# A gated mix of an S4 convolution and linear attention: key sums through DMA transposes and narrow matmuls, values copied once to bf16, the query normaliser read back repeated from DRAM, the cosine table from ScalarE, and a new order

## The chip, the cores and the metric

One core of a Trainium2 chip. A core has engines with in-order queues of their own: TensorE (PE in the profile; PEld is its weight loads), VectorE (DVE), ScalarE (ACT), GpSimd (POOL) and SyncE (SP, which here issues nearly all DMAs). The metric is device time in microseconds (us) of one execution; the numbers shown are medians over runs. A time in the profile comes from one profiled execution.

## The reference

Two branches read the same `x = A_u` (2,048 positions, 512 channels, bf16) and are mixed by a gate per position:

```python
g = _sigmoid((x * gate_w).sum(-1, keepdims=True))
a = _A_ref(x, A_A_re, A_A_im, A_B_re, A_B_im, A_C_re, A_C_im, A_log_dt, A_Dskip)
b = _B_ref(x, B_wqkv, B_w_phi, B_wo)
return g * a + (1 - g) * b
```

Branch A (`_A_ref`) is an S4 layer: for each channel `d` a kernel `K[d, l] = Re sum_n C[d,n] exp(dt[d] A[d,n] l) dt[d] B[d,n]` over 128 states, a causal convolution of `x` with `K` by FFT of length 4,096, and `+ u * Dskip`. Branch B is linear attention with 32 heads of 16:

```python
phi_q = jnp.concatenate([_softmax(pq, axis=-1), _softmax(-pq, axis=-1)], axis=-1)
phi_k = jnp.concatenate([_softmax(pk, axis=-1), _softmax(-pk, axis=-1)], axis=-1)
kv = jnp.einsum("bhsf,bhsd->bhfd", phi_k, v)
z  = jnp.einsum("bhsf->bhf", phi_k)
num = jnp.einsum("bhqf,bhfd->bhqd", phi_q, kv)
den = jnp.einsum("bhqf,bhf->bhq", phi_q, z)[..., None] + 1e-6
o = num / den
```

and `o @ wo`, where `pq` and `pk` are the queries and keys times a 16 x 16 matrix of each head.

## The kernel before

**The order.** Nothing is scheduled by hand in the text. One `Plan` object (L92) collects the work as nodes: `P.add(engine, cost, function, deps, take, drop)` for a few instructions of one engine, `P.dma(...)` for DMAs that SP issues. The numbers (cost, `move`) served a planner outside the program; in the program the sequence of all nodes is the string `ORDER` (two digits of base 64 each), `SIDES` says for every node that copies a PSUM tile out ("eviction", function `evict`, L546) whether ScalarE or VectorE does it, and `RINGS` which PSUM ring a matmul's output takes. `run` (L165 on) calls the node functions in that sequence, and every engine executes its share in order. `take` and `drop` count buffers: the numbers in the dictionary at L1364 (`"Ek": 2`, `"bs": 3` ...) are how many of each exist.

**Start.** `prepare` (L267) loads and transposes weights by `DMA_TRANSPOSE` from DRAM (`turn` L299, wTk L303, xT L310), loads `u` in 16 pieces (UD, L1298), and builds the tables of sines and cosines. `trig` (L332) makes one: GpSimd writes the indices (L344), VectorE multiplies (L345) and masks to 13 bits (L346), ScalarE takes the sine (L347). TB, the largest with 2,048 columns, is made so twice, as a sine and as a cosine (L360). The state tables (Ctab, Dtab, stat) and the forward FFT of `u` (XAu, XU, XUd in DRAM) are made here too.

**Keys** (L671 to L733): eight sets of two tiles (`u` = 0, 1) of 128 positions. Per tile: `pk`, 4 matmuls; `ex`, two exponentials Ek of 128 x 512 on ScalarE, for the signs + and -; `rd` (L693), VectorE sums Ek over the 16 features of each head into Zk; per set `ln`, ScalarE makes 1/Zk as exp(-ln) into the last two columns of `vr`; `pv`, the values vp into PSUM; `sc` (L717), VectorE multiplies the values, straight from PSUM in f32, by 1/Zk, once for each sign, into vr; `kn` (L726), 32 narrow matmuls add Ek^T vr to kvp. Behind the last set stand `f1` (L797 to L811: zj, zcol, KVbd, SSw) and Mw, which folds `kv` with `wo`.

**Queries** (L849 to L954): four blocks of 512 positions. Per block: `pq`, `qe` (Eq, 128 x 512, 8 of them), `zz` (sums by matmuls), z1 to z5 (logarithms and exponentials on ScalarE, sums on VectorE; lnZ, den), which end in `apm`: the factor of each (head, position). As each head has 16 rows of Eq, `apm` must be repeated 16 times over the partitions: `pe` (L920) does this with matmuls by the selection matrix Xsel into PSUM (aexp), and `de` (L925) multiplies Eq by it, 128 x 512 at a time; `pbm` (L935) multiplies by Mw, `bs` evicts, `bd` stores to bSd in DRAM.

**Filter and convolution**, eight parts `h`, spread between all this. `plan_tables` (L738): args by matmul, E (two exponentials) and cs (two sines) on ScalarE, each 128 x 1,024. `kgen` (L962): A (L975, 128 x 2,048), R (L982, L985, two halves each of two) on VectorE, kps by many 32-column matmuls (L212), KD evicted, psA by matmul, XA evicted. `transform` (L1048): U loaded, psB, XK evicted, t = U x XK on VectorE, psz, Zr evicted and stored to Zd in DRAM, ZT read back, psy, bS (mixed with the gate), and the stores of the output (L1203).

**Tables of ScalarE.** Exponentials and logarithms use one function table, sines another; going from one to the other is an `ACT_TABLE_LOAD` (L75).

Of the kernel before, what the change touches and what calls it, by code (L numbers as in the profile page):

```python
# [91 lines left out]
class Plan:  # L92
# [1336 lines left out]
```

## Time and profile before

| | before |
|---|---|
| median of 8 runs | 319.88 us (318.15 to 321.77) |
| the profiled execution | 321.77 us, its span 320.0 us |
| TensorE busy | 234.3 us (73%) |
| VectorE busy | 271.5 us (85%) |
| ScalarE busy | 228.9 us (72%) |
| DMA | 37.53 MB |

The same page shows the span in 40 slices of 8 us; each digit is the busy share in tenths (9 is 90% or more), PEclk the granted clock of TensorE in tenths, DMA the busy share of its 16 engines:

```profile
PE   0044656549899697797999899999979835695830
...
DVE  8977999988999999989699999999898949966240
ACT  2549999989898986768796999998474598333100
...
PEclk9999958556999999799599999999999985587785
DMA  8999989556000000400213006206557699288533
```

Start, keys, queries and tail can be seen in it: DMA is busy for the first ten slices, then hardly for six; TensorE is full from slice 20 on; behind slice 31 all engines have gaps. A row of the groups reads: line, engine, operation, output <- inputs, shape and type, count | busy us, mean ns of one | idle us before them <- what ended it. Neighbours overlap by a few tens of ns, so busy time divided by count is a little less than the mean.

### The profile page before, as it was taken

To read this page: it belongs to the slowest core of one execution; us is meant where nothing else is said; L and a number is where in the kernel's file an instruction comes from. 1 tells how busy PE (TensorE), PEld (TensorE's weight loads), DVE (VectorE), ACT (ScalarE), POOL (GpSimd) and SP (SyncE) were. 2 spreads that over 40 slices of the span, in tenths; PEclk is the share of its full clock that TensorE was granted. 3 is DMA by queue.
4 is the path that set the end of the run, shared out by engine and by line. 5 is a ranking of instruction groups with operands and counts; after the bars stand their busy time and mean duration, and the time that the engine had idled before them with its cause. 6 is when DMAs were issued, how large, how long until landed. Compare 5 with 4: busy or idle time off the path is not lost. (4 is left out here: it accounts for less than half of the span.)

```text
span 320.0 us, 10544 instructions
## 1 busy us (share of the span) xinstructions
PE 234.3 (73%) x4680; PEld 138.1 (43%) x4680; DVE 271.5 (85%) x432; ACT 228.9 (72%) x302; POOL 9.1 (3%) x23
## 2 busy tenths in 40 slices
PE   0044656549899697797999899999979835695830
PEld 0044645435344255364356544645554313454720
DVE  8977999988999999989699999999898949966240
ACT  2549999989898986768796999998474598333100
POOL 9000000000000001000000000000000000000000
PEclk9999958556999999799599999999999985587785
DMA  8999989556000000400213006206557699288533
GB/s 143 189 115 221 268 142 191 207 190 199 0 3 2 4 2 4 131 4 3 66 26 97 20 35 179 71 20 213 166 142 217 180 267 234 81 229 183 104 71 74
DMA packets 85293, 37.53 MB, mean 117 GB/s; under 512 B 68480, under 2 KB 81920, under 8 KB 85248
## 3 DMA queue, kind: packets, MB, share of 16 engines
q1 hardware_dynamic: 82080, 36.34, 48.0%
q10 hardware_dynamic: 3168, 0.52, 0.9%
q8 instruction: 36, 0.59, 0.8%
q14 instruction: 9, 0.07, 0.1%
HBM read 20.34 MB, written 14.68 MB: 109 GB/s over the span
## 5 line engine op out<-in xcount | busy, mean ns | idle before, releaser
L975 DVE TENSOR_TENSOR A<-Ctab,Dtab 128x2048 bf16<-128x2048 bf16 x32 | 38.4, 1217 | 0.7 <-PE kps L212 0.7
L83 ACT ACTIVATE E<-args 128x1024 bf16<-128x1024 f32 x32 | 30.8, 1023 | 7.6 <-PE args L754 7.6
L574 PE MATMUL psA<-W,UD 128*64 128x256 bf16 x128 | 14.6, 390 | 25.3 <-DMA nBre<-in_A_B_re_dram 20.6
L935 PE MATMUL bps<-Mw,Eq 128*128 128x512 bf16 x128 | 32.1, 396 | 0.0
L83 ACT ACTIVATE cs<-args 128x1024 bf16<-128x1024 f32 x32 | 30.4, 1056 | 1.8 <-PE args L772 1.7
L212 PE MATMUL kps<-R,A 128*32 128x64 bf16 x1536 | 26.8, 227 | 6.2 <-DVE R L985 2.3
L212 PEld LDWEIGHTS <-A 128*32 128x32 bf16 x1536 | 24.8, 152 | 12.0 <-issue 7.5
L982 DVE TENSOR_TENSOR R<-E,cs 128x1024 bf16<-128x1024 bf16 x32 | 21.9, 684 | 4.3 <-ACT cs L83 4.3
L574 PEld LDWEIGHTS <-UD 128*64 128x64 bf16 x128 | 12.4, 206 | 27.2 <-issue 27.1
L925 DVE TENSOR_TENSOR Eq<-Eq,aexp 128x512 bf16<-128x512 bf16 x32 | 20.6, 681 | 3.3 <-PE aexp L920 2.9
L225 PE MATMUL psB<-XAu,TB 64*128 64x128 bf16 x256 | 13.4, 278 | 12.6 <-ACT XU L555 8.2
L985 DVE TENSOR_TENSOR R<-E,cs 128x1024 bf16<-128x1024 bf16 x32 | 22.0, 688 | 0.6
L83 ACT ACTIVATE Eq<-pq 128x512 bf16<-128x512 f32 x32 | 17.2, 602 | 3.8 <-issue 2.5
L717 DVE TENSOR_TENSOR vr<-vp,vr 128x512 bf16<-128x512 f32 x32 | 19.6, 680 | 0.0
L693 DVE TENSOR_REDUCE Zk<-Ek 128x64 f32<-128x1024 bf16 x16 | 18.8, 1212 | 0.8 <-ACT Ek L83 0.6
L555 ACT CAST Zr<-psz 128x1024 bf16<-128x1024 f32 x13 | 13.3, 1023 | 8.2 <-PE psz L1115 8.2
L1101 DVE TENSOR_TENSOR t<-U,XK 128x1024 bf16<-128x1024 bf16 x28 | 17.9, 684 | 0.6 <-ACT XK L555 0.5
L935 PEld LDWEIGHTS <-Eq 128*128 128x128 bf16 x128 | 11.6, 100 | 15.6 <-issue 3.5
L713 PE MATMUL vp<-Wv,xT 128*128 128x512 bf16 x64 | 15.8, 379 | 3.3 <-DVE vr L717 3.3
L225 PEld LDWEIGHTS <-TB 64*128 64x128 bf16 x256 | 11.6, 125 | 14.4 <-issue 12.5
L83 ACT ACTIVATE Ek<-pk 128x512 bf16<-128x512 f32 x32 | 16.7, 609 | 0.7 <-PE pk L681 0.6
L681 PE MATMUL pk<-Wkp,xT 128*128 128x512 bf16 x64 | 17.0, 405 | 0.2 <-ACT Ek L83 0.2
(179 smaller groups left out, 488.2 us busy)
## 6 DMA issues: line engine op xcount, KB each, us to landing
XUd<-XU SPq DMA_DIRECT2D x4, 1024.0 KB, 5.3
U<-XUd SPq DMA_DIRECT2D x16, 256.0 KB, 3.1
U<-XUd SPq DMA_DIRECT2D x32, 128.0 KB, 3.3
Zd<-Zr SPq DMA_DIRECT2D x14, 256.0 KB, 2.8
ZT<-Zd SPq DMA_DIRECT2D x6, 512.0 KB, 7.3
UD<-in_A_u_dram SPq DMA_DIRECT2D x16, 128.0 KB, 4.1
xr<-in_A_u_dram SPq DMA_DIRECT2D x1, 2048.0 KB, 10.0
bSd<-bs SPq DMA_DIRECT2D x16, 128.0 KB, 2.7
```

What stands on the lines that cost most here:

```text
L83: i = self.nc.scalar.activation(**kw)
L212: nc.tensor.matmul(kps[32 * dj:32 * dj + 32, g4, e, :], lhsT=A[q][:, o, :, :, d].rearrange("p a b -> p (a b)"), rhs=R[ri][:, d, :], start= ...
L225: nc.tensor.matmul(ps[:, e, sl, :], lhsT=fc.TB[rows, r, 1 - ri:3 - ri, :].rearrange("p a b -> p (a b)"), rhs=XA[rows, r, ri, :], start=(ri ...
L574: nc.tensor.matmul(box.ps[64 * e:64 * e + 64, i, :], lhsT=g.UD[:].rearrange("p t (e g) -> p g e t", e=2)[:, gw * h + 4 * g4 + i, e, :], rh ...
L693: nc.vector.tensor_reduce(out=K.Z[:, u, :, :], in_=K.E[:, u, :, :].rearrange("p g (h f) -> p g h f", f=16), axis=mybir.AxisListType.X, op= ...
L717: nc.vector.tensor_tensor(out=K.v[:, u, sg, :, 0:32].rearrange("p m (h e) -> p m h e", e=16), in0=box.ps[:].rearrange("p (m h e) -> p m h ...
L925: nc.vector.tensor_tensor(out=e, in0=e, in1=box.ps[:], op=ALU.mult)
L935: nc.tensor.matmul(box.ps[:], lhsT=Q.e[:, m, sg, 128 * i:128 * i + 128], rhs=g.Mw[:, 4 * sg + m, :], start=(k == 0), stop=False, skip_grou ...
L975: nc.vector.tensor_tensor(out=c.A[q][:].rearrange("p o a b d -> p (o a) b d"), in0=Ct.to_broadcast([128, 8, 8, 32]), in1=Dt.to_broadcast([ ...
L982: nc.vector.tensor_tensor(out=c.R[o][:, :, 32:64], in0=E[:, :, 32:64], in1=x, op=ALU.mult)
L985: nc.vector.tensor_tensor(out=c.R[o][:, :, 0:32], in0=E[:, :, 0:32], in1=x[:, :, ::-1], op=ALU.mult)
L1101: nc.vector.tensor_tensor(out=o[:, k], in0=box.U[:, k], in1=box.XK[:].rearrange("p s (o d) -> p o s d", o=no), op=ALU.mult)
```

## The change

1. **Key sums.** `et` issues, for each of 16 key tiles, a `DMA_TRANSPOSE` of Ek (256 KB) from SBUF to SBUF into ET; `rd` is then 8 matmuls per tile with ET as the weights and 8 columns of the selection matrix SZ, into a PSUM bank. `ln` reads that bank into `lk`, and writes 1/Zk as one row of `vr`, whose layout becomes (17, 32). Ek has three buffers in place of two, ET two.
2. **Values.** `ve`, a new eviction, copies vp once from PSUM to bf16 `vb`, with head and element exchanged; `sc` is one multiply of 128 x 1,024 bf16 per tile, for both signs. `f1` and `kn` read the new layout.
3. **Query normaliser.** `wz` writes apm to DRAM (`apd`, four DMAs per block), `ax` reads it back with each row repeated 16 times (aexp, four DMAs of 256 KB per block, two buffers), and `de` is four multiplies of 128 x 1,024 bf16 per block. The matmuls `pe` and Xsel are gone.
4. **Cosine table.** TB's cosine is made on ScalarE from the sine's argument: Abs, then Sin with an offset of half pi.
5. **Buffers.** KD 2 to 1, bs 3 to 2; XA of the last two parts is one tile.
6. **Order.** ORDER, SIDES and RINGS are new, for the new nodes and, all through, for the old. Wide evictions (1,024 columns) on VectorE go from 18 to 27; the narrow bs from 6 to 3.

```diff
-    ORDER = ("0g0J1000010K070o0b09050O0T110P120Q0L0M0d0R0N020h080m060c14190X04130e0r0f030i0n0p0j0k0l0S0U150V0Y160Z0q0s0W1e170-181a1b"
...
+    ORDER = ("020m0J0O0P000g0d010o0p0-0Q0_070r0h040e0f0n0s0K09120q0R0L0t03130j14150b0M0N100T0U0V11170W0X1c0S1618191d0Z1e1a1b2E1f1g0i"
...
-    xcol = wp.tile([128, 4, 8], F32, name="xcol")
-    iota_f(nc, xcol[:], [[8, 4], [1, 8]])
-    at.Xsel = wp.tile([128, 4, 128], BF16, name="Xsel")
...
-    for i, o in ((0, SIN), (1, COS)):
-        trig(lambda i=i: tb(i), 2048, p63, lambda o=o: o, 1, [[2, 32], [128, 64]], f"TB{i}")
+    trig(lambda: tb(0), 2048, p63, lambda: SIN, 1, [[2, 32], [128, 64]], "TB0")
+    w0 = lambda: F.v[0][:].bitcast(F32).rearrange("p (r i) -> p r i", i=64)
+    S(1.9, lambda: nc.scalar.activation(out=w0(), in_=F.v[0][:].rearrange("p (r i) -> p r i", i=64), func=ACT.Abs, scale=2.0 * PI_S / 8192.0, bias=F.mpi[:]), w="v0")
+    S(1.9, lambda: act(out=tb(1), in_=w0(), func=ACT.Sin, scale=-1.0, bias=HALF_PI), r="act v0", w="TB1")
...
-                    K.E = g.kwk.tile([128, 2, 2, 512], BF16, name="Ek", tag="Ek")
+                    K.E = g.kwk.tile([128, 2, 2, 512], BF16, name="Ek", tag="Ek", bufs=3)
...
+            def et(u=u, K=K):
+                if u == 0:
+                    K.T = g.kwk.tile([128, 2, 8, 128], BF16, name="ET")
+                nc.sync.dma_start(out=K.T[:, u], in_=K.E[:, u, :, :].rearrange("p g x -> p (g x)"), transpose=True)
+
             def rd(u=u, K=K):
                 if u == 0:
-                    K.Z = g.kwk.tile([128, 2, 2, 32], F32, name="Zk")
-                nc.vector.tensor_reduce(out=K.Z[:, u, :, :], in_=K.E[:, u, :, :].rearrange("p g (h f) -> p g h f", f=16),
-                                        axis=mybir.AxisListType.X, op=ALU.add)
+                    K.Z = g.psA.tile([128, 2, 2, 4, 8], F32, name="Zk", tag="bk")
+                for i in range(8):
+                    nc.tensor.matmul(K.Z[:, u, i // 4, i % 4, :], lhsT=K.T[:, u, i, :], rhs=at.SZ[:, 0, 0:8], start=True, stop=True)
...
-            K.v = g.kwk.tile([128, 2, 2, 16, 34], BF16, name="vr")
-            act(out=K.Z[:], in_=K.Z[:], func=ACT.Ln)
-            act(out=K.v[:, :, :, :, 32:34], in_=K.Z[:].rearrange("p u g (m h) -> p (u g) m h", h=2), func=ACT.Exp, scale=-1.0)
+            K.v = g.kwk.tile([128, 2, 2, 17, 32], BF16, name="vr")
+            K.L = g.kwk.tile([128, 2, 2, 32], F32, name="lk", bufs=1)
+            act(out=K.L[:], in_=K.Z[:].rearrange("p u g m h -> p u g (m h)"), func=ACT.Ln)
+            act(out=K.v[:, :, :, 16, :], in_=K.L[:], func=ACT.Exp, scale=-1.0)
...
+            def ve(box=box):
+                box.v = g.kwk.tile([128, 16, 32], BF16, name="vb", bufs=2)
+                i = box.ps[:].rearrange("p (h e) -> p e h", e=16)
...
             def sc(u=u, K=K, box=box):
-                for sg in range(2):
-                    nc.vector.tensor_tensor(out=K.v[:, u, sg, :, 0:32].rearrange("p m (h e) -> p m h e", e=16),
-                                            in0=box.ps[:].rearrange("p (m h e) -> p m h e", m=16, h=2),
-                                            in1=K.v[:, u, sg, :, 32:34].unsqueeze(3).to_broadcast([128, 16, 2, 16]), op=ALU.mult)
-                box.ps = None
+                nc.vector.tensor_tensor(out=K.v[:, u, :, 0:16, :], in0=box.v[:].unsqueeze(1).to_broadcast([128, 2, 16, 32]),
+                                        in1=K.v[:, u, :, 16, :].unsqueeze(2).to_broadcast([128, 2, 16, 32]), op=ALU.mult)
...
-                                         rhs=K.v[:, u, sg, 4 * m + pr, :], start=(st == 0 and i == 0), stop=(st == 15),
+                                         rhs=K.v[:, u, sg, :, 8 * m + 2 * pr:8 * m + 2 * pr + 2], start=(st == 0 and i == 0), stop=(st == 15),
...
+        def wz(b=b, Q=Q):
+            for i in range(4):
+                nc.sync.dma_start(out=g.apd[b, :, :, 128 * i:128 * i + 128], in_=Q.apm[32 * i:32 * i + 32, :, :])
+            Q.apm = None
...
+            def ax(b=b, m=m, box=box):
+                box.x = g.qp.tile([128, 2, 512], BF16, name="aexp", bufs=2)
+                nc.sync.dma_start(out=box.x[:], in_=g.apd[b, 8 * m:8 * m + 8].unsqueeze(1).to_broadcast([8, 16, 2, 512]))
+
+            def de(m=m, box=box, Q=Q):
+                nc.vector.tensor_tensor(out=Q.e[:, m], in0=Q.e[:, m], in1=box.x[:], op=ALU.mult)
+                box.x = None
...
-                def pe(i=i, mp=mp, box=box, Q=Q):
-                    box.ps = g.psA.tile([128, 2, 2, 128], F32, name="aexp", tag="bk")
...
-                box.b = g.qp.tile([128, 512], BF16, name="bs", bufs=3)
+                box.b = g.qp.tile([128, 512], BF16, name="bs", bufs=2)
...
-            K.KD = g.wk.tile([128, 2, 4, 128], BF16, name="KD", bufs=2)
+            K.KD = g.wk.tile([128, 2, 4, 128], BF16, name="KD", bufs=1)
...
-        P = Plan({"XAu": 1, "Ek": 2, "Zk": 2, "vr": 2, "acc": 1, "r8": 2, "nrm": 1, "bs": 3, "E": 4, "cs": 4, "A": 3, "R": 3, "KD": 2, "XA": 2,
+        P = Plan({"XAu": 1, "Ek": 3, "ET": 2, "vr": 2, "vb": 2, "acc": 1, "r8": 2, "nrm": 1, "ax": 2, "bs": 2, "E": 4, "cs": 4, "A": 3, "R": 3, "KD": 1, "XA": 2,
```

How the order moves, at three places. First ScalarE's queue at the start of the keys, before; a set has four key exponentials.

```order
L75 ACT_TABLE_LOAD
L83 ACTIVATE Ek<-pk 128x512 x2
L83 ACTIVATE gz<-gz 128x16
L83 ACTIVATE Ek<-pk 128x512 x6
L83 ACTIVATE Zk<-Zk 128x128
L83 ACTIVATE vr<-Zk 128x64x2
L83 ACTIVATE E<-args 128x32x32 x2
L83 ACTIVATE Zk<-Zk 128x128
```

And now, at the same place:

```order
L83 ACTIVATE Ek<-pk 128x512 x12
L83 ACTIVATE E<-args 128x32x32 x2
L83 ACTIVATE lk<-Zk 128x128
L83 ACTIVATE vr<-lk 128x4x32
L83 ACTIVATE E<-args 128x32x32 x4
L83 ACTIVATE lk<-Zk 128x128
L83 ACTIVATE vr<-lk 128x4x32
L83 ACTIVATE Ek<-pk 128x512 x2
L83 ACTIVATE E<-args 128x32x32 x2
L83 ACTIVATE Ek<-pk 128x512 x2
```

Twelve exponentials (three sets of four) stand ahead of the first logarithm, and E of the filter between the sets; before it were eight, two sets.

Second, VectorE's queue around the normaliser of a query block (lnZ and den are z2 and z4; t is the convolution's product), before:

```order
L893 TENSOR_TENSOR lnZ<-lnZ,zrow 128x256
L553 CAST XA<-psA 128x64x16
L900 TENSOR_TENSOR lnZ<-lnZ,den 128x256
L975 TENSOR_TENSOR A<-Ctab,Dtab 128x2048
L925 TENSOR_TENSOR Eq<-Eq,aexp 128x4x128 x5
L1101 TENSOR_TENSOR t<-U,XK 128x1024 x2
```

And now, at the first place where the multiplies by aexp stand:

```order
L914 TENSOR_TENSOR lnZ<-lnZ,den 128x256
L550 CAST Zr<-psz 128x2x8x64
L991 TENSOR_TENSOR A<-Ctab,Dtab 128x2048
L998 TENSOR_TENSOR R<-E,cs 128x32x32
L1000 TENSOR_SCALAR cs<-cs 128x1024
L1001 TENSOR_TENSOR R<-E,cs 128x32x32
L991 TENSOR_TENSOR A<-Ctab,Dtab 128x2048
L1117 TENSOR_TENSOR t<-U,XK 128x1024 x2
L939 TENSOR_TENSOR Eq<-Eq,aexp 128x1024 x2
L905 TENSOR_TENSOR den<-zs,den 128x256
```

Between the last step of the normaliser and the first multiply stood one A; now there are eight instructions of the filter and the convolution.

Third, SP's queue, of the changed kernel, where a block's normaliser is written and read back (Zd is the convolution's store, U its load, bSd the store of a block's result):

```order
L927 DMA apd<-apm 64x1x128 x4
L1141 DMA Zd_0_117<-Zr 128x1024 x2
L936 DMA aexp<-apd 128x1x1024 x4
L1084 DMA U<-XUd 128x2x512
L1086 DMA U<-XUd 64x2x512 x2
L1084 DMA U<-XUd 128x2x512
L1086 DMA U<-XUd 64x2x512 x2
L927 DMA apd<-apm 64x1x128 x4
L966 DMA bSd<-bs 128x4x128
```

Before, SP had only the U, Zd and bSd of these rows; the apd and aexp rows are new, and the loads of U now stand behind them.

133 lines of the change are left out of this document (67 added, 66 removed).

## The prediction

> **What bounds the kernel now.** I read the head of the page first, then the windows of four stages, then the groups of instructions, the timeline at the seams, and the DMA issues. Rows are copied whole; "..." marks rows left out between them. Columns of a window: its length, then busy time and instructions of each engine, granted clock, DMA share, GB/s.
>
> ```profile
> span 320.0 us, 10544 instructions
> PE 234.3 (73%) x4680; PEld 138.1 (43%) x4680; DVE 271.5 (85%) x432; ACT 228.9 (72%) x302; POOL 9.1 (3%) x23
> ...
> 77.23 1.08 ACT L83 ACTIVATE Ek<-pk 128x512 bf16<-128x512 f32 x2
> ...
> 127.03 0.11 DVE L801 TENSOR_TENSOR zj<-kvp,mask 128x16 f32<-128x16 f32 x1
> ...
> 247.89 0.69 DVE L925 TENSOR_TENSOR Eq<-Eq,aexp 128x512 bf16<-128x512 bf16 x1 [0.49 <-PE aexp L920]
> ...
> core 0: us, PE busy (x) PEld busy (x) DVE busy (x) ACT busy (x) POOL busy (x), PEclk, DMA share, GB/s
> 0.00:77.00 77.00, 35.79 (x486) 30.04 (x487) 67.98 (x144) 60.43 (x71) 8.17 (x22) 0.80 0.92 191
> 77.00:127.00 50.00, 44.03 (x913) 21.08 (x912) 49.04 (x65) 42.22 (x72) 0.95 (x1) 1.00 0.02 6
> 127.00:249.00 122.00, 113.65 (x2052) 61.49 (x2051) 112.32 (x175) 97.17 (x131) 0.00 (x0) 0.96 0.32 92
> 249.00:320.00 71.00, 40.85 (x1234) 25.49 (x1231) 42.18 (x51) 29.07 (x30) 0.00 (x0) 0.73 0.68 158
> ...
> 160.00:180.00 20.00, 20.00 (x528) 12.28 (x526) 19.72 (x32) 17.26 (x24) 0.00 (x0) 1.00 0.23 57
> ```
>
> The first key exponential (77.23), the first instruction behind the key sums (127.03) and the last query multiply (247.89 + 0.69 = 248.6) cut the run into start 77.2, keys 49.8, queries 121.5 and tail 71.5 us; these add to the span of 320.0. VectorE is the limit of the keys stage: 49.0 of 50 us. In the queries stage it shares that with TensorE, 112.3 beside 113.7 of 122, and from 160 to 180 TensorE has no gap at all. So VectorE time saved pays in full only where TensorE and ScalarE are not just behind. In the tail no engine is full.
>
> **The change part by part.** First the prices.
>
> ```profile
> L693 DVE TENSOR_REDUCE Zk<-Ek 128x64 f32<-128x1024 bf16 x16 | 18.8, 1212 | 0.8 <-ACT Ek L83 0.6
> ...
> L717 DVE TENSOR_TENSOR vr<-vp,vr 128x512 bf16<-128x512 f32 x32 | 19.6, 680 | 0.0
> ...
> L925 DVE TENSOR_TENSOR Eq<-Eq,aexp 128x512 bf16<-128x512 bf16 x32 | 20.6, 681 | 3.3 <-PE aexp L920 2.9
> ...
> L982 DVE TENSOR_TENSOR R<-E,cs 128x1024 bf16<-128x1024 bf16 x32 | 21.9, 684 | 4.3 <-ACT cs L83 4.3
> ...
> L984 DVE TENSOR_SCALAR cs<-cs 128x1024 bf16<-128x1024 bf16 x16 | 6.8, 427 | 0.6
> ...
> L975 DVE TENSOR_TENSOR A<-Ctab,Dtab 128x2048 bf16<-128x2048 bf16 x32 | 38.4, 1217 | 0.7 <-PE kps L212 0.7
> ...
> L553 DVE CAST XK<-psB 128x1024 bf16<-128x1024 f32 x3 | 3.7, 1220 | 2.3 <-PE psB L1079 2.3
> ...
> L553 DVE CAST bs<-bps 128x512 bf16<-128x512 f32 x6 | 4.1, 685 | 2.5 <-PE bps L938 2.5
> ...
> L83 ACT ACTIVATE E<-args 128x1024 bf16<-128x1024 f32 x32 | 30.8, 1023 | 7.6 <-PE args L754 7.6
> ...
> L83 ACT ACTIVATE cs<-args 128x1024 bf16<-128x1024 f32 x32 | 30.4, 1056 | 1.8 <-PE args L772 1.7
> ...
> L555 ACT CAST XA<-psA 128x1024 bf16<-128x1024 f32 x13 | 13.2, 1029 | 4.8 <-PE psA L1025 4.8
> ...
> L75 ACT ACT_TABLE_LOAD x12 | 15.4, 1283 | 0.9 <-PEq L1413 0.7
> ...
> L212 PE MATMUL kps<-R,A 128*32 128x64 bf16 x1536 | 26.8, 227 | 6.2 <-DVE R L985 2.3
> ...
> L772 PE MATMUL args<-selE,stat 64*128 64x512 bf16 x32 | 10.6, 415 | 5.2 <-ACT cs L83 3.8 <-ACT E L83 0.6 <-ACT Zr L555 0.3
> ...
> L1025 PE MATMUL psA<-W,KD 128*128 128x256 bf16 x64 | 10.4, 299 | 2.8 <-ACT KD L555 2.3 <-DVE KD L553 0.4
> ...
> L641 PE MATMUL gps<-gw,xT 128*128 128x1 bf16 x64 | 1.9, 166 | 0.0
> ...
> L660 PE MATMUL zps<-xT,gwr 128*32 128x512 bf16 x16 | 1.9, 626 | 1.1 <-ACT E L83 1.1
> ...
> L1115 PE MATMUL psz<-t,TI 128*128 128x512 bf16 x56 | 16.1, 415 | 0.9 <-DVE t L1101 0.8
> ...
> L920 PE MATMUL aexp<-apm,Xsel 32*128 32x256 bf16 x64 | 10.7, 283 | 0.9 <-ACT apm L83 0.9
> ```
>
> Busy time divided by count is what one costs beside its neighbours. The pivot of the change is the rows of L717, L925 and L982: a multiply over 512 columns with an operand in PSUM takes 0.68 us, one over 1,024 bf16 columns out of SBUF 0.684. Halving the number of instructions at that price halves the time.
>
> **Keys.** VectorE loses 16 sums (18.8) and 32 multiplies (19.6); it gains 13 value copies (0.685: 8.9) and 16 wide multiplies (0.684: 10.9). The new order also brings filter work forward into this stage: 8 more A (9.7), 16 more R (10.9), 4 negations (1.7) and two 1,024-wide evictions (2.4). 49.0 - 38.4 + 44.5 = 55.1 us. ScalarE gets 6 E (0.96 each: 5.8), 8 cosines (7.6), 2 table loads (2.6), three wide evictions (3.1) and two value copies (1.3, at VectorE's price): 42.2 + 20.4 = 62.6. TensorE gets 512 kps (17.4 ns each: 8.9), 12 psA (2.0), 14 args (4.6) and 128 eight-column matmuls; the nearest row to these is gps, the same weights with one column, 30 ns: 3.8. The zps (1.9) move out. 44.0 + 19.3 - 1.9 = 61.4. So this stage gets **longer**: its limit passes to ScalarE and TensorE. With the limiting engine 0.98 busy, as VectorE was, it takes 62.6 / 0.98 = 63.9; with 0.88, as TensorE was, 61.4 / 0.88 = 69.8. Three engines so close will not all be full; I take **67**.
>
> Whether the key sums come in time depends on 16 transposes on SP that read from SBUF, which the trace does not show. The bounds are the transposes that it shows:
>
> ```profile
> 0.73 1.24 SPq L299 DMA_TRANSPOSE nCre<-in_A_C_re_dram  x1
> ...
> 5.54 2.80 SPq L303 DMA_TRANSPOSE wTk<-in_B_wqkv_dram  x1
> ...
> wTk<-in_B_wqkv_dram SPq DMA_TRANSPOSE x1, 5.0
> ```
>
> 1.24 us of SP for 128 KB, 2.80 for 512 KB; on the line between them 256 KB takes 1.8 us, and landing up to 5.0. Times 16 that is 20 to 45 us of a 67 us stage in which SP and DMA otherwise have nothing (DMA share 0.02). A set's sums are late by 5.0 + 1.8 us against the reduce; the third Ek buffer and the new row order (12 key exponentials and two E, some 8 us at 0.52 and 0.96, ahead of the first logarithm) cover it. I cost it at nothing. That cover is gone when one transpose keeps SP over 65 / 16 = 4.1 us.
>
> **Queries.** TensorE loses the 64 aexp matmuls (10.7), 512 kps (8.9), 12 psA (2.0) and 6 args (2.0), gains zps (1.9) and eight psz (2.3): 113.7 - 19.4 = 94.3. VectorE loses 32 multiplies (20.6), 8 A (9.8), 16 R (10.9), 4 negations (1.7), four t at R's price (2.7) and a bs (0.7), gains 16 wide multiplies (10.9) and four evictions on balance (4.9): 112.3 - 30.6 = 81.7. ScalarE falls from 97.2 by five XA, one XK, one KD, four cosines and one table load, less four bs and one Zr, to about 88. TensorE stays the limit; at its share of before, 113.65 / 122 = 0.93, 94.3 gives 101. I take **100**.
>
> The normaliser's way is new: four writes of apd, four reads of aexp per block, in SP's order.
>
> ```profile
> 150.55 0.43 ACT L83 ACTIVATE apm<-lnZ 128x256 bf16<-128x256 f32 x1
> ...
> 151.03 0.59 PE L920 MATMUL aexp<-apm,Xsel 32*128 32x256 bf16 x6
> ...
> pz<-pt SPq DMA_DIRECT2D x4, 128.0 KB, 2.2
> ...
> U<-XUd SPq DMA_DIRECT2D x16, 256.0 KB, 3.1
> ...
> ZT<-Zd SPq DMA_DIRECT2D x6, 512.0 KB, 7.3
> ```
>
> Before, TensorE takes apm up 0.5 us after ScalarE starts it. Now a write (2.2 us like pz, behind four issues of about half a microsecond) and a 256 KB read (3.1 like U) stand between: about 7.5 us. In the new order VectorE has a Zr, two A, two R, a negation and two t, 6.8 us by the rows above, between its last normaliser step and the first multiply of a block, so it waits a microsecond or two per block, out of 18 us that it has to spare. Behind the waiting multiply stand t and the next normaliser steps; behind the waiting SP stand the U loads and the Zd writes. Bounds for one read: 3.1 (U) and 7.3 (ZT, twice the bytes); I take U, the same bytes.
>
> The Trainium skill, page "DMA: Bandwidth & Descriptors", section "Why a DMA increments its semaphore by 16 and not by 1", speaks against this read: a DMA is spread over the largest number of engines up to 16 that divides the slowest dimension of both its sides, and the read's source has 8 there, so eight engines carry it, not sixteen. No row of before shows such a read; if the rule holds here, the sum is that of the second rival and not this one.
>
> **Tail.** Of its 6 E, 8 cosines and 2 table loads, all but 4 cosines and one load move ahead, and so goes the one long stall of VectorE:
>
> ```profile
> 260.07 0.69 DVE L982 TENSOR_TENSOR R<-E,cs 128x1024 bf16<-128x1024 bf16 x1 [4.32 <-ACT cs L83]
> ```
>
> 4.3 us off; four more t (2.7) fall into VectorE's idle 29 us. 71.5 becomes **67**; next late are the loads of ZT, as before.
>
> **Start.** The second table loses two VectorE passes of 2,048 (the one below, and the argument pass at a like price) and gains one ScalarE pass of about 2.0:
>
> ```profile
> L346 DVE TENSOR_SCALAR tgv<-tgv 128x2048 int32<-128x2048 int32 x2 | 2.4, 1222 | 0.0
> ```
>
> VectorE is 0.88 busy here, so some of 2.4 us shows, but u's loads now stand behind the weights' on SP: 77.2 becomes **76**, bounds 74 and 78. The halved XA and KD and the bs buffers cost nothing while TensorE's next matmuls of another kind cover their evictions; gone, that is an eviction's 1.2 us eight times, 10 us at most.
>
> **Sum.** 76 + 67 + 100 + 67 = 310 of span, 10 less than 320.0. The profiled execution took 321.77 us, 1.8 over its span; the median, 319.88, is 1.9 under that. So 310 it is, against the median.
>
> **Rivals.** *TensorE is the real limit* and VectorE's relief is not passed on. For it: 20.00 of 20 in the window above, and six aexp in 0.59 us, so the 64 take only some 6.4 us from the queue; against: the gaps beside it in the other stages. Keys 70, queries (113.65 - 15.1) / 0.93 = 106, tail 68: 320, and 316 with half of it. *The normaliser's round trip shows*: with reads of 5 to 7.3 us the first multiply of each of four blocks is 2 to 4 us later, the second buffer pair as much again: 4 to 8 us beyond the forecast, 314 to 318. *The transposes out of SBUF set the keys stage* (the slower side): for it, nothing in the trace has read SBUF with a transpose, and every set waits on it; against, 1.24 to 2.80 us. It decides from 4.1 us of SP each; at 5.5 us the stage is 16 x 5.5 = 88, the time 331; at 5, 323. *The saving does not come about* (wide multiply not at 0.684): 16 + 16 x 0.68 more on VectorE, hidden in the keys, half seen in the queries: 316, within the first rival's band.
>
> **How the numbers follow.** Forecast 0.57, its own range 303 to 315; TensorE limit 0.16 (316 to 320); round trip 0.12 (314 to 318); transposes 0.15 (over 320). The range runs from 298 (keys at 63.9, queries without the share of idle, 95) to 325 (a transpose of 5 us); outside lie the dearest transposes and a start still better. About 0.5%, 1.6 us, is what a measurement can tell from no change. Faster (under 318.3): 0.57, half the first rival, most of the second, 0.72. Same: 0.11. Slower: 0.17, the transposes and a little of the first.
>
> **What would show it.** Right: Zk sums and aexp matmuls gone; vr and Eq near 0.68 at half the count; keys 64 to 70 us with ScalarE and TensorE over 0.9; VectorE near 0.82 busy in the queries; no 4 us stall on cs in the tail. Wrong: ScalarE's lk waiting for Zk and SP's queue full from ET to ET; Eq waiting over 2 us for aexp's DMA; U, ZT or Zd later because SP waits; kvp or the copies dearer for their strided reads (bounds, equal and double: 512 kvp at kps's price, 0 to 9 us of TensorE; the copies, 0 to 9 of VectorE; both in the keys stage and in the range).

## The result: slower by 3%, and the profile after

The changed kernel takes 330.49 us (median of 11 runs, 327.07 to 334.5) beside 319.48 us for the kernel before (32 runs by then): a ratio of 1.032 (95% interval 1.029 to 1.036). Forecast was 310, with 298 to 325 as the range. The ratio leaves out the longer executions of both kernels, and both profiles are of such a one (334.5 us, span 332.7; before 321.77): in the kernels below that share its code the start came out about 1 us shorter, the keys 1 to 3, the queries 2 to 4, and the tail within 1 us of it.

The seams in the timeline of the changed kernel, the windows between them (columns as before), and three rows of its groups:

```profile
81.12 1.08 ACT L83 ACTIVATE Ek<-pk 128x512 bf16<-128x512 f32 x2 [1.22 <-PE pk L678]
...
154.02 0.17 DVE L815 TENSOR_TENSOR zj<-kvp,mask 128x16 f32<-128x16 f32 x1
...
257.77 0.69 DVE L939 TENSOR_TENSOR Eq<-Eq,aexp 128x1024 bf16<-128x1024 bf16 x1 [0.72 <-DMA aexp<-apd]
```

```profile
0.00:81.10 81.10, 34.25 (x485) 28.59 (x486) 64.47 (x141) 62.55 (x72) 8.33 (x20) 0.80 0.82 174
81.10:154.00 72.90, 64.27 (x1454) 35.06 (x1452) 54.65 (x77) 62.15 (x92) 0.95 (x1) 0.94 0.41 84
154.00:257.00 103.00, 90.77 (x1556) 48.70 (x1556) 82.96 (x127) 79.08 (x111) 0.00 (x0) 0.93 0.46 131
257.00:332.70 75.70, 43.46 (x1250) 27.06 (x1250) 46.46 (x57) 22.07 (x25) 0.00 (x0) 0.75 0.70 165
```

```profile
L939 DVE TENSOR_TENSOR Eq<-Eq,aexp 128x1024 bf16<-128x1024 bf16 x16 | 11.0, 690 | 13.5 <-DMA aexp<-apd 13.5
...
L731 DVE TENSOR_TENSOR vr<-vb,vr 128x1024 bf16<-128x1024 bf16 x16 | 10.8, 690 | 4.6 <-ACT vr L83 4.1
...
L550 DVE CAST vb<-vp 128x512 bf16<-128x512 f32 x14 | 9.5, 686 | 10.2 <-PE vp L722 10.2
```

| stage | before | forecast | changed |
|---|---|---|---|
| start, to the first Ek | 77.2 | 76 | 81.1 |
| keys, to zj | 49.8 | 67 | 72.9 |
| queries, to the end of the last Eq | 121.5 | 100 | 104.4 |
| tail | 71.5 | 67 | 74.2 |

Most of the work came out as costed. VectorE is busy 248.5 us in place of 271.5, its keys stage 54.65 (forecast 55.1), ScalarE's 62.15 (62.6), TensorE's 64.27 (61.4); the wide multiplies take 0.69 us. Yet each stage of this profile is 4 to 7 us longer than forecast: what was missed is idle time, not work. Keys and queries together take 177.3 us beside 171.3, with 24 us less of VectorE in them.

Three waits stand out in the view of waits, and two in SP's (us in total, times, longest):

```profile
DVE Eq L939 <- DMA aexp<-apd: 13.5, 12, 1.7
...
PE psy L1190 <- DMA ZT<-Zd: 9.2, 2, 5.7
...
PE psA L571 <- DMA UD<-in_A_u_dram: 8.0, 1, 8.0
...
SPq L1219 <- DMA out_dram<-bS: 11.8, 2, 10.8
SPq L936 <- DMA aexp<-apd: 8.7, 6, 2.3
```

The first three are loads that SP issues, too late (UD, ZT) or too slow (aexp). The last two are from SP's own view: twice it waited with a store for an earlier store to land, and six times with a read of aexp for an earlier read.

### The profile page after: what moved, and what is told of

The parts are those of the page before. It is cut to its first block, busy times and chain, and to the rows that moved or that the text cites. A ratio compares the mean times of both kernels' runs of the same rounds, so it can differ in the third digit from the quotient of the medians.

```text
span 332.7 us, 10733 instructions
## 1 busy us (share of the span) xinstructions
PE 232.8 (70%) x4744; PEld 139.4 (42%) x4744; DVE 248.5 (75%) x401; ACT 225.9 (68%) x299; POOL 9.3 (3%) x21
## 4 chain that ended last, share of the span: by engine, by line
PE 29%; DVE 25%; DMA 13%; ACT 11%; SPq 11%; issue 7%; DVEq 0%; ACTq 0%
DMA aexp<-apd 7%; PE pk L678 5%; DVE A L991 4%; PE kps L214 4%; DVE R L998 3%; ACT XAu L552 3%; PE psA L571 3%; PE vp L722 3%; SPq L294 3%; DVE R L1001 3%; SPq L1312 2%; DVE XA L550 2%; DMA U<-XUd 2%; PE psz L1163 2%; DVE t L1117 2%
## 5 line engine op out<-in xcount | busy, mean ns | idle before, releaser
L951 PE MATMUL bps<-Mw,Eq 128*128 128x512 bf16 x128 | 30.9, 380 | 1.3 <-DVE Eq L939 1.2
L571 PE MATMUL psA<-W,UD 128*64 128x256 bf16 x128 | 13.9, 375 | 12.8 <-DMA UD<-in_A_u_dram 8.0
L1131 PE MATMUL psz<-t,TI 128*128 128x512 bf16 x56 | 16.5, 410 | 7.3 <-DVE t L1117 4.7
L939 DVE TENSOR_TENSOR Eq<-Eq,aexp 128x1024 bf16<-128x1024 bf16 x16 | 11.0, 690 | 13.5 <-DMA aexp<-apd 13.5
L1211 DVE TENSOR_TENSOR bS<-psy,gT 128x1024 bf16<-128x1024 f32 x7 | 8.5, 1219 | 16.6 <-PE psy L1190 16.6
L678 PE MATMUL pk<-Wkp,xT 128*128 128x512 bf16 x64 | 19.6, 450 | 0.0
L951 PEld LDWEIGHTS <-Eq 128*128 128x128 bf16 x128 | 11.4, 98 | 16.7 <-DVE Eq L939 3.0
L722 PE MATMUL vp<-Wv,xT 128*128 128x512 bf16 x64 | 18.1, 412 | 0.1
L571 PEld LDWEIGHTS <-UD 128*64 128x64 bf16 x128 | 11.6, 205 | 15.0 <-issue 14.8
L552 ACT CAST Zr<-psz 128x1024 bf16<-128x1024 f32 x11 | 11.2, 1017 | 9.8 <-issue 7.7
L874 PE MATMUL pq<-xT,Wqp 128*128 128x512 bf16 x64 | 17.3, 410 | 0.0
```

Of the source, the lines that this page charges most:

```text
L552: nc.scalar.copy(out=o, in_=i)
L571: nc.tensor.matmul(box.ps[64 * e:64 * e + 64, i, :], lhsT=g.UD[:].rearrange("p t (e g) -> p g e t", e=2)[:, gw * h + 4 * g4 + i, e, :], rh ...
L678: nc.tensor.matmul(box.ps[:], lhsT=xT[:, kt, ss], rhs=g.Wkp[:, kt, :], start=(kt == 0), stop=(kt == 3))
L722: nc.tensor.matmul(box.ps[:], lhsT=xT[:, kt, ss], rhs=g.Wv[:, kt, :], start=(kt == 0), stop=(kt == 3))
L874: nc.tensor.matmul(box.ps[:], lhsT=g.Wqp[:, kt, 128 * m:128 * m + 128], rhs=xT[:, kt, 512 * b:512 * b + 512], start=(kt == 0), stop=(kt == 3))
L951: nc.tensor.matmul(box.ps[:], lhsT=Q.e[:, m, sg, 128 * i:128 * i + 128], rhs=g.Mw[:, 4 * sg + m, :], start=(k == 0), stop=False, skip_grou ...
```

## Experiments

Ratios are to the kernel before, with their 95% intervals; the changed kernel's is 1.032. "Stage" lengths come from each kernel's own profile.

### Which wait costs what

**ZT ahead of the stores.** The nodes of the last two ZT loads (1053, 1056) moved ahead of the stores in `ORDER`. SP's rows:

```diff
 L1150 DMA ZT<-Zd_0_119 64x32x128 x2
+L1150 DMA ZT<-Zd_0_120 64x32x64 x2
 L1219 DMA out_dram<-bS_5186 32x8x128 x4
...
-L1150 DMA ZT<-Zd_0_120 64x32x64
```

> The changed kernel with one edit on SP's queue: the last part's two loads of ZT are issued ahead of 12 stores of the output, not between and behind them. Theory W (what was lost is waiting on loads that SP issues late): in the changed kernel the last psy waited 9.2 us for ZT and the last bS 9.7 us for that psy, so the run gets 4 to 7 us shorter, about 324 in place of 329, ratio to before 1.01 to 1.02. Rival E (the engines are full, so a wait removed shifts to the next): under 1.5 us. Rival S (the stores themselves end the run): ZT early, last bS early, but the time within 1.5 us.

Measured 328.6, 1.024 (1.018 to 1.030): 2.7 us by the ratios, between theories W and S; the interval just overlaps the changed kernel's. SP's timeline, first of the changed kernel, then of this one, with its wait for a store:

```profile
296.63 2.62 SPq L1150 DMA_DIRECT2D ZT<-Zd  x2
299.36 17.26 SPq L1219 DMA_DIRECT2D out_dram<-bS  x8
316.71 0.58 SPq L1150 DMA_DIRECT2D ZT<-Zd  x1
317.39 2.79 SPq L1219 DMA_DIRECT2D out_dram<-bS  x4
320.22 0.58 SPq L1150 DMA_DIRECT2D ZT<-Zd  x1
```

```profile
292.87 8.57 SPq L1150 DMA_DIRECT2D ZT<-Zd  x4
301.54 22.67 SPq L1219 DMA_DIRECT2D out_dram<-bS  x24
...
SPq L1219 <- DMA out_dram<-bS: 8.0, 1, 8.0
```

In the changed kernel one store held SP for 10.8 us, as it waited for an earlier store, and both ZT loads stood behind it. With them ahead the last bS ends 58.7 us after the last Eq and not 67.6, but then the stores end the run: a store still holds SP for 8.0 us, and the run ends 13.6 us behind the last bS, not 6.6. The tail is 72.4 us, where 67 was forecast. What the stores alone cost was not tested.

**The start, first try.** The same for the SP queue's head alone (C's transposes, UD, wTk ahead of the rest).

> The changed kernel with the start of SP's queue put as it was before: C's transposes, the first UD loads, wTk, the other UD loads, then the rest. Theory W: psA starts near 21 us and not at 32, the first Ek comes 3 to 5 us earlier (76 to 78 in place of 81), and the run is 3 to 5 us shorter, ratio 1.015 to 1.025. Rival E (VectorE's and ScalarE's table work bounds the start): the first Ek within 1.5 us of where it was, the time the same.

Measured 336.1, 1.047 (1.041 to 1.053): worse, and a badly chosen edit. TensorE's rows at its start:

```profile
24.06 1.01 PE L523 MATMUL wps<-Wphi,wTk 128*128 128x128 bf16 x8 [24.06 <-DVE Wphi L240]
29.29 1.89 PE L611 MATMUL wps<-Wphi,wTq 128*128 128x128 bf16 x16 [4.22 <-DMA wTq<-in_B_wqkv_dram]
30.97 1.06 PE L523 MATMUL wps<-Wphi,wTk 128*128 128x128 bf16 x8
31.96 1.12 PE L571 MATMUL psA<-W,UD 128*64 128x256 bf16 x8
```

In the new order TensorE has wps ahead of psA; wps needs the small weight loads that the edit pushed back, so psA, whose u is loaded early now, still starts at 32 us. Here one queue of the order could not be moved alone.

**The start, all queues.** The first 256 nodes on every engine in the order of before, evictions on the engines and into the PSUM rings of before.

> The changed kernel with its first 256 nodes (all ahead of the keys) in the order of before, on every engine, and their evictions on the engines of before. The first Ek stood at 77.2 before and at 80 to 81 in the changed kernel. If the start's order is what cost that: first Ek at 76 to 77.5, TensorE's clock up earlier for the first pk, the run 3 to 6 us shorter, ratio 1.013 to 1.023. If the new cosine or the load of the DMA queues cost it: within 1.5 us of the changed kernel.

Measured 326.0, 1.019 (1.014 to 1.025). psA starts at 20.5 us, the first Ek stands at 76.4, as the theory had it. The first psA of the kernel before, of the changed kernel, and of this one:

```profile
20.64 3.68 PE L574 MATMUL psA<-W,UD 128*64 128x256 bf16 x32 [20.64 <-DMA nBre<-in_A_B_re_dram]
...
31.98 5.17 PE L571 MATMUL psA<-W,UD 128*64 128x256 bf16 x56 [8.04 <-DMA UD<-in_A_u_dram]
...
20.52 3.68 PE L571 MATMUL psA<-W,UD 128*64 128x256 bf16 x32 [20.52 <-DMA nBre<-in_A_B_re_dram]
```

So the new order of the start costs 4 us. The cosine from ScalarE stays in, and no gain of it shows: in the six kernels here that have it with the start of before, the first Ek stands at 76.4 to 77.7 us, in the four with both tables made the old way at 76.6 to 77.2.

**No wait for aexp.**

```diff
-tensor_tensor(out=Q.e[:, m], in0=Q.e[:, m], in1=box.x[:], op=ALU.mult)
+tensor_tensor(out=Q.e[:, m], in0=Q.e[:, m], in1=g.Mw[:, 0:2, :], op=ALU.mult)
```

> The changed kernel, but the 16 Eq multiplies take a tile of Mw in place of aexp (the normaliser is not applied); apd is written and aexp is read by DMA as before, only nobody waits. Theory W: VectorE's 13.5 us of waits for aexp go; with what they pull behind them the run is 6 to 13 us shorter, ratio 0.99 to 1.01. Rival E (TensorE, 0.88 busy in this stage, takes over): 0 to 4 us.

The multiplies then apply no normaliser. Measured 323.0, 1.008 (1.005 to 1.011): 7.8 us. The queries take 96.3 us. Theory W.

**No wait for the transposes.** The narrow matmuls' weights are `K.E[:, u, i // 4, 128 * (i % 4):...]`, not `K.T[:, u, i, :]`, so the sums are not the key sums.

> The changed kernel, but the 128 narrow matmuls take Ek itself as weights in place of ET (the sums run over positions, not features); the 16 transposes are still issued, nobody waits for them. Theory T (my slower-side rival, that transposes out of SBUF are dear): the keys stage of 73 us falls by over 5 us, the run by 5 or more, ratio 1.015 or less. Theory E (the stage is bound by TensorE and ScalarE, each near 62 to 64 us busy in it): within 2 us of 329, ratio 1.027 to 1.037.

Measured 329.7, 1.028 (1.023 to 1.034), keys 72.2: theory E. The slower-side rival of the prediction is refuted. The transposes of the changed kernel (duration on SP, min/median/max):

```profile
L690 SPq DMA_TRANSPOSE ET<-Ek x16: 1231/1234/1908, 82.2 to 138.0; - x16
```

1.23 us of SP each, where 1.8 was taken and 4.1 was the point of danger.

**Another order of repetition in the read.** Each row then gets the factor of another head.

```diff
-g.apd[b, 8 * m:8 * m + 8].unsqueeze(1).to_broadcast([8, 16, 2, 512])
+g.apd[b, 8 * m:8 * m + 8].unsqueeze(0).to_broadcast([16, 8, 2, 512])
```

> The changed kernel with another order of repetition in the reads of aexp: the source's slowest dimension is 16 repeats, then 8 heads, in place of 8 heads, then 16 repeats (each row of Eq gets the factor of another head). Same bytes. If a DMA is spread over the largest divisor up to 16 of that dimension (the Trainium skill), 16 engines carry each read and not 8: the reads land 1 to 2 us earlier, VectorE's waits for aexp fall from some 12 to under 7 us, the run is 2 to 5 us shorter, ratio 1.013 to 1.025. If the read is no slower for its eight engines: waits and time the same, ratio 1.028 to 1.034.

Measured 326.9, 1.022 (1.010 to 1.033): 3.5 us by the ratios, but the interval overlaps the changed kernel's. The waits, forecast at under 7 us:

```profile
DVE Eq L939 <- DMA aexp<-apd: 7.2, 10, 1.4
```

The queries take 95.7 us, as without any wait (96.3), where the changed kernel and five others with its queries and waits took 100.6 to 104.4; by these profiles the waits that are left no longer lengthen the stage. The chain that ended last holds five reads, here of 4.20, 4.32, 4.31, 3.22 and 3.68 us, in the changed kernel of 4.34, 4.31, 5.23, 3.56 and 4.48. So the Trainium skill's rule on the spread of a DMA (page "DMA: Bandwidth & Descriptors", section "Why a DMA increments its semaphore by 16 and not by 1") points the right way; the landing falls by up to 0.9 us, not by half, and the time by less than the queries stage. No view shows how many engines carried a read, so that this is the reason is not shown.

### What the relief of VectorE is worth

**In the order of before.** Reduces over one of 16 features, one of two Eq multiplies left out:

```diff
-in_=K.E[:, u, :, :].rearrange("p g (h f) -> p g h f", f=16),
+in_=K.E[:, u, :, :].rearrange("p g (h f) -> p g h f", f=16)[:, :, :, 0:1],
...
+                    if mp == 0:
                         nc.vector.tensor_tensor(out=e, in0=e, in1=box.ps[:], op=ALU.mult)
```

> The kernel before in its own order, with about the VectorE work taken away that the change takes away: each key sum covers one of 16 features, and of each pair of Eq multiplies one is left out (some 17 + 10 us of VectorE, in its full stages). Theory P (TensorE was just behind VectorE: busy 157.7 of the 171.3 us of keys and queries, so relief of VectorE is not passed on): 4 to 12 us shorter, ratio 0.96 to 0.99. Theory D (as the prediction had it, the relief passes on and only the new order or its DMAs lose it): 17 to 26 us shorter, ratio 0.92 to 0.95.

Measured 312.8, 0.979 (0.970 to 0.988): 6.6 us for some 23 us of VectorE (138.3 busy in keys and queries, 161.4 before). This is the main finding on the sum: a quarter or a little more of the relief passes on (17 to 41% by the interval), even without a single new DMA.

**Less TensorE.** `range(4)` to `range(2)` over the parts of pk, vp and pq, in the changed kernel and in the kernel before, there alone and with the lighter VectorE:

> The changed kernel with half the products in pk, vp and pq (two of four parts of the 512 channels are left out): 96 matmuls of 512 columns less, about 25 us of TensorE, 17 of them in the keys stage and 8.5 in the queries. Theory P (TensorE limits): keys 72 falls to 60 to 64, queries by 4 to 8, the run 12 to 20 us shorter, ratio 0.97 to 0.99. Theory A (ScalarE limits the keys stage, the aexp waits the queries): keys 68 or more, the run under 7 us shorter, ratio over 1.007.

> The kernel before with half the products of pk, vp and pq left out (96 matmuls of 512 columns, about 25 us of TensorE), VectorE's work whole. Theory P (TensorE just behind VectorE): VectorE, 161 us busy of the 171 in keys and queries, does not let it show: 0 to 7 us shorter, ratio 0.978 to 1.0. If TensorE alone set the stages: 12 us shorter or more, ratio under 0.965.

> Both at once on the kernel before: the VectorE work of before_light gone (which alone gave 6.5 us) and half of pk, vp and pq too. Theory P: each covers the other, so together they give clearly more than the two alone added: 15 to 22 us shorter, ratio 0.93 to 0.955. Rival A (ScalarE and the order's dependences are the next limit): about the sum of the two, 8 to 13 us, ratio 0.96 to 0.975.

Measured 1.014 (1.007 to 1.021), 0.998 (0.993 to 1.003) and 0.975 (0.963 to 0.987). The changed kernel falls by some 6 us, all of it in the keys (65.8), a quarter of the 25 us that the products left out were put at: by the time theory A, by the stage between the two. On the kernel before TensorE's relief alone gives nothing (its busy time in the two stages falls by 16 us, and its granted clock in the keys is 0.74, not 1.00), and on top of VectorE's it gives 1.3 us, with intervals that overlap: rival A. The keys stage of before, lighter on VectorE, then on both:

```profile
76.60:122.60 46.00, 43.64 (x904) 21.39 (x909) 35.52 (x66) 41.14 (x71) 0.95 (x1) 0.94 0.02 4
...
77.10:120.30 43.20, 34.98 (x850) 15.59 (x849) 34.78 (x66) 40.70 (x71) 0.95 (x1) 0.85 0.02 5
```

49.8 us with VectorE full, 46.0 with TensorE next (43.6 busy), 43.2 with ScalarE next (40.7): three engines one behind the other. The queries go from 121.5 to 117.6 and 116.7 with no engine over 0.91 busy. But the kernel with TensorE's relief alone, as slow as before, has 117.5 us there too, so these profiles do not show that the queries passed on anything of VectorE's relief. What binds them, the order's dependences or something else, was not settled.

### The work and the order apart

**One part back at a time, in the new order.** `rd` back to `tensor_reduce` at the place of the transpose; or aexp back to matmuls with Xsel and multiplies of 512 out of PSUM, at the place of the second and fourth multiply.

> The changed kernel and its order with the key sums back on VectorE (16 reduces, 18.8 us more there), no transposes and no narrow matmuls (5.7 us less on TensorE). Theory P: VectorE has 18 us of idle in the keys stage and TensorE is relieved, so the time stays within 3 us of 329 (ratio 1.02 to 1.04): the key sums' new way is worth about nothing. Theory D: VectorE's 18.8 us come back on the path, 8 us longer or more, ratio over 1.05.

> The changed kernel and its order with the query normaliser back on TensorE (64 aexp matmuls, 10.7 us busy more, 32 multiplies of 512 out of PSUM, 9.7 us more on VectorE), no apd and no aexp DMAs. The waits for aexp, worth 7.7 us by the run without them, go. Theory P with waits: TensorE's added matmuls cost 4 to 10 us, so the time stays between 3 us less and 4 us more than 329. If the new order alone were at fault: the same as with the DMAs. If the round trip were the whole loss: 7 us or more shorter, ratio 1.01 or less.

> The new order with both round trips taken back: key sums by VectorE's reduce, normaliser by matmuls and narrow multiplies out of PSUM. By the two runs that took back one each (9 us and 15 us longer than the changed kernel, in different stages) the two add: 350 to 356 us, ratio 1.095 to 1.115. If the parts stand in for one another (the limit passes to TensorE or ScalarE once one is back) it is 340 to 347.

Measured 1.058 (1.048 to 1.067), 1.080 (1.072 to 1.088), and both 1.105 (1.099 to 1.111), which is 353.8 us: they add. Only the stage concerned moves: keys 81.4, queries 116.3. Theory P had the key sums at nothing and was wrong: in this order VectorE's 18.8 us come back on the path, for 8 of them. For the normaliser none of the three forecasts had 15 us more. So the two DMA routes do earn 8 and 15 us, but against an order that without them, with the rest of the change, is 34 us worse than the old one; and the old operations stand there at places made for the new.

**The new work in the old order**, and the rest of the change alone in the old order (nodes that both have keep their sequence, the others stand where what they read is ready; KD's and bs's fewer buffers push some nodes back):

> All the new work of the changed kernel, put in the order of the kernel before: every node that both have stands where it stood, a transpose follows its exponential at once, the narrow matmuls stand ahead of the logarithm, the copy ahead of its multiply, the four wide Eq multiplies where the first narrow ones stood. Theory O (the new order is what loses; the new work is good): 8 us or more shorter than the changed kernel, ratio to before 1.005 or less. Theory R (the new work has two round trips by DMA, 7 us each, which only another order can cover): ScalarE waits for Zk in each of 8 sets and VectorE some 5 us for aexp in each of 4 blocks, so no shorter than the changed kernel: ratio 1.03 or more.

> The order of before with only the rest of the change: values copied once to bf16, cosine table from ScalarE, KD with one buffer, bs with two, XA of the last parts in one tile; key sums and query normaliser as before. The prediction put all of these at nothing beside a microsecond at the start: within 2 us of before, ratio 0.99 to 1.006. Rival B (the buffers taken away make TensorE wait for evictions): 3 to 10 us longer, ratio 1.01 to 1.03.

Measured 400.1, 1.250 (1.244 to 1.256), and 367.9, 1.150 (1.144 to 1.157). The second says little of the edits it was meant for: its reduces stand at the place of the transposes and not where the old order had them, and nodes were pushed back for KD's one buffer. Its queries take 149.9 us; which of these made them so long was not separated. So it fails as a test of the values and the buffers, which stay unmeasured alone. The first has that too, but its waits show the round trips uncovered:

```profile
DVE Eq L939 <- DMA aexp<-apd: 50.5, 16, 9.8
...
ACT lk L83 <- PE Zk L696: 17.0, 8, 3.8
```

50.5 us for aexp in place of 13.5: theory R. At these places the old order does not cover the new work; the new order could not simply be left off.

### The repairs together

> The changed kernel with the three repairs: the start in the order of before, ZT's last loads ahead of the stores, and apm written twice (8 writes per block, not 4), so that the reads' source has a slowest dimension of 16. The first two gave 3.2 and 2.6 us alone. If they add and the reads gain 2 to 4 less 2 for the added writes: 321 to 325, ratio 1.005 to 1.018. It does not beat the kernel before unless the reads' waits go altogether.

> The start in the order of before, ZT's last loads behind the next 8 stores but ahead of the other 16, and the reads of aexp with 16 repeats as the slowest dimension (rows get the factor of another head). If the three losses add: 329.3 less 3.2, less 1 to 2.6, less 2.4 to 6 is 318 to 322, ratio 0.995 to 1.01: the distance to before is then these three. If they overlap (one wait hides the other): 323 to 326, ratio 1.012 to 1.02.

> As three16, but with apd holding each row twice, so that the right factors are read with a slowest dimension of 16; written by four DMAs per block, one for each sign and copy, whose target has 4 as its slowest dimension. If the writes land about as before (2 us): 319 to 323, ratio 0.998 to 1.012. If their four engines or small pieces make them slow (3 us or more): 322 to 326, ratio 1.008 to 1.02.

The first writes apd twice by 8 DMAs per block, the third by 4:

```diff
-            for i in range(4):
-                nc.sync.dma_start(out=g.apd[b, :, :, 128 * i:128 * i + 128], in_=Q.apm[32 * i:32 * i + 32, :, :])
+            for c in range(2):
+                for s in range(2):
+                    nc.sync.dma_start(out=g.apd[b, :, c, s, :].rearrange("h (i t) -> i h t", i=4), in_=Q.apm[:, s, :])
...
+g.apd[b, 8 * m:8 * m + 8].rearrange("h c s q -> (h c) s q").unsqueeze(1).to_broadcast([16, 8, 2, 512])
```

Measured 1.017 (1.008 to 1.026), 1.003 (0.998 to 1.009) and 0.993 (0.988 to 0.997). With 8 writes VectorE waits 11.4 us for aexp, with 4 only

```profile
DVE Eq L940 <- DMA aexp<-apd: 5.6, 9, 1.0
```

and the queries take 94.9 us. So the start's order and the order of repetition in the reads are most of the distance to before (2.9 of 3.2% in the second, whose queries take 96.4 us beside 102.8 with the repaired start alone, 1.019). The last ZT loads in these two kernels stand behind 8 stores again, and TensorE still waited 6.9 and 6.4 us for ZT, so that gain is hardly in it. The last kernel is the fastest of those that do the whole work of the change: its median is 319.8 us beside 320.0, by the ratio it is 0.3 to 1.2% faster. With the two so far apart I call it level with the kernel before, not faster (its forecast was 0.998 to 1.012).

## Why the prediction was wrong, point by point

Forecast was 310, measured 330. By the profile the start is 5 us over its forecast, the keys 6, the queries 4 and the tail 7.

- **What bounds the kernel: right.** The prediction said that relief pays in full only where no other engine is just behind, and in the keys put ScalarE and TensorE as the new limit. The lighter kernels show just that for the keys, 49.8, 46.0, 43.2. For the queries it is not shown.
- **The sums of work: right but for one.** In the keys within 1 us on VectorE and ScalarE and 3 us on TensorE, whose granted clock was 0.94 there and 1.00 before; in the queries VectorE 83.0 (81.7), TensorE 90.8 (94.3), ScalarE 79.1, where 88 was wrong: fewer cosines and evictions fall into the stage than were counted. It bound nothing.
- **Keys, 67: mis-sized.** The step "three engines so close will not all be full; I take 67" set the limiting engine at 0.94 busy. It was 64.27 of 72.9, 0.88, the share that the prediction had named as its other bound, and with 3 us more of TensorE. (In the kernels that share this stage it takes 69.9 to 72.3 us.) The costing of the transposes at nothing was right (zk_const).
- **Queries, 100: the step on the normaliser failed.** "It waits a microsecond or two per block, out of 18 us that it has to spare" holds for the first multiply of each block: 1.69, 1.38, 1.24 and 0.67 us, 5.0 in all. The sum had nothing for the other three reads, which come one behind another through two buffers: the later multiplies waited another 8.5 us. The first block:

```profile
186.98 0.69 DVE L939 TENSOR_TENSOR Eq<-Eq,aexp 128x1024 bf16<-128x1024 bf16 x1 [1.69 <-DMA aexp<-apd]
188.54 0.69 DVE L939 TENSOR_TENSOR Eq<-Eq,aexp 128x1024 bf16<-128x1024 bf16 x1 [0.86 <-DMA aexp<-apd]
...
191.35 0.68 DVE L939 TENSOR_TENSOR Eq<-Eq,aexp 128x1024 bf16<-128x1024 bf16 x1
193.60 0.69 DVE L939 TENSOR_TENSOR Eq<-Eq,aexp 128x1024 bf16<-128x1024 bf16 x1 [1.57 <-DMA aexp<-apd]
```

  Together that is 13.5 us, 12 times out of 16, and those waits were on the path, for 7.8 us (aexp_const). A full engine's average idle is no cover for a wait at a fixed place of its queue. I took 3.1 us for a read by U's row; the chain had 3.6 to 5.2. The second rival (4 to 8 us, with later pairs late too) was the true mechanism here, and another order of repetition repaired part of it (aexp16). That the stage comes to 100.6 to 102.8 us in the kernels that share it, near the 100 of the forecast, is luck: TensorE is busy 5 to 8 us less there than its sum, which offsets most of the waits.
- **Start, 76: the step on SP's order failed.** "u's loads now stand behind the weights' on SP" was seen and bounded at 78. psA began 11 us later than before, and 4 us of it reached the first Ek (old_start). The microsecond that the cosine was to gain does not show in any run.
- **Tail, 67: one step right, one missed.** The stall on cs went: up to VectorE's last R (which ends at 281.6 before, 286.7 now) the tail has 28.2 us, 33.0 before. From there to the end it has 46.0 us, 38.4 before. Two sentences of the step failed. "Four more t (2.7) fall into VectorE's idle 29 us": where they stand VectorE is full,

```profile
258.50:288.00 29.50, 20.10 (x400) 11.25 (x403) 29.19 (x39) 15.03 (x17) 0.00 (x0) 0.77 0.89 215
```

  And "next late are the loads of ZT, as before" hid the loss. Before, the store that holds SP stands behind the last ZT load:

```profile
299.28 0.58 SPq L1134 DMA_DIRECT2D ZT<-Zd  x1
299.90 17.45 SPq L1203 DMA_DIRECT2D out_dram<-bS  x16
...
SPq L1203 <- DMA out_dram<-bS: 5.8, 1, 5.8
```

  In the new order it stands ahead of the last two and holds SP longer, 10.8 us. I counted how many DMAs the step issues and did not read what stands ahead of them in the queue. The repair gave 2.7 of the 7 us between forecast and profile; why the stores wait so long stays open.
- **The rivals.** Dear transposes: refuted; the chance of a slower kernel rested mostly on them, and it came out slower for other reasons. TensorE as the limit: too simple; on the kernel before its relief alone is worth nothing, and about 16 of the 23 us of VectorE's relief are lost to both other engines and, it seems, to the order. The round trip: right, and not alone. Wide multiplies dearer than costed: refuted by their 0.690 us. No rival had several small losses at once, and that is what the runs point to: 4.2 us for the start, 2.7 for ZT, 3.5 to 7.8 for aexp, against 6.6 us of gain in the kernel of before_light. These do not add up to the 10 us between the kernels exactly; the rest, the stores and the filter work moved into the keys among it, has no run of its own.

## What to carry to other kernels

When several engines are each 0.8 to 0.95 busy, cost a relief by the next engine, not by what is taken away: here about a quarter was passed on. A round trip by DMA that replaces an operation is hidden only by work that stands between its issue and its use in the consumer's own queue; count that work at each place, for every read and not only the first, and don't offset the wait against average idle time. Where an order is new, read each queue's rows at the start and the end of the program too, SP's above all: a load behind a store that waits is as late as the store.

## What the runs showed of the hardware that was not expected

Near the end one 64 KB store held SP for 10.8 us, as it waited for an earlier store, and 5.8 us in the kernel before, whose DMA issues show 2.2 us to landing for the median of them. The same bytes read from DRAM with 8 or 16 as the source's slowest dimension cost VectorE 11.8 to 14.5 us of waits over 16 reads in the one case (the seven kernels that wait for reads like those of the changed one), 5.6 to 7.8 in the other with four writes (aexp16, three16, best2), but 11.4 with eight writes (best). And a transpose of 256 KB from SBUF to SBUF takes SP 1.23 us, no more than one of 128 KB out of DRAM at the start (1.24).
